# A written-out order for a fused attention and feed-forward kernel: both sketch loads first, and every engine's list rearranged

## The chip, the cores and the metric

The kernel runs on one core of one Trainium2 chip. The metric is the device time of one execution in microseconds (us). The engines are TensorE (PE), VectorE (DVE), ScalarE (ACT), GpSimd (POOL) and SyncE (SP), which only issues DMAs here; ACT issues a few as well.

## The reference

Polynomial-sketch attention, then a feed-forward block on its output. Batch 4, 4 heads, 1088 tokens, head size 32, sketch rank 8, model width 128, hidden width 512.

```python
def phi(x):                                  # sketch features, 8 x 8 = 64 for each token
    a = einsum('rd,bhsd->bhsr', S1, x)
    b = einsum('rd,bhsd->bhsr', S2, x)
    return einsum('bhsi,bhsj->bhsij', a, b).reshape(..., 64)
q_p, k_p = phi(q), phi(k)
kv  = einsum('bhsf,bhsd->bhfd', k_p, v)
z   = sum(k_p, axis=2)
num = einsum('bhsf,bhfd->bhsd', q_p, kv)
den = einsum('bhsf,bhf->bhs', q_p, z)[..., None] + 1e-06
x   = (num / den), heads side by side        # (4, 1088, 128)
xn  = (x - mean(x)) / sqrt(var(x) + 1e-06) * g_ln
out = x + maximum(xn @ w_ch1, 0) @ w_ch2
```

S1, S2, g_ln and the two weights reach the chip as 64-bit floats where numpy made them so, and are put together as 32-bit floats by integer and float steps on the engines (the `w_` steps).

## The kernel before

The kernel is a set of small steps (functions marked `@op`) and a text, `PROGRAM`, that lists 498 of them in order with their arguments. Nothing else schedules: each step issues its instructions to its engine's list when the text comes to it, so the text sets the order on every engine and in SP's DMA queue. An engine works through its list in order. A letter among the arguments names the engine (V for VectorE, A for ScalarE, G for GpSimd, S for SP); the last numbers of a step that uses TensorE are its banks of PSUM (0 to 7, in the tile `ALL`).

The four batches go through the same stages, and the text interleaves the stages of different batches.

- **Opening.** `ld_s` loads the two sketches into `s_raw` (8 rows), `ld_w` the weights, `ld_g` the norm's gain. `c_ones`, `c_small` (`one`, `m896`), `c_iota` (`row`, `head`), `c_masks` (six VectorE instructions that make `m32`, `m8` and `m2` from `row` and `head`), `c_ident`, `c_pads`, `c_vpad` and `c_rest` write constants. `fill n w z` is a matmul of ones with ones, w columns wide, whose result nobody reads.
- **Floats from 64 bits.** For sketch (0), first (1) and second weight (2): `w_ex`, `w_bits`, `w_e2`, `w_mant`, `w_low`, `w_e3`, `w_add` or `w_addlow`, and `w_mul`; for the sketch `s_heads` writes `s_f` at the end. `w_e2` and `w_mant` on ScalarE read `m896` and `one`. `sk` (L367, L369) turns the sketches on TensorE, `sk_8`, `sk_d`, `sk_2`, `sk_r`, `sk_q` copy them out. `fold` (L352) folds gain and mean into the first weight, `fold_cp` copies it.
- **Keys of a batch.** `ld S k b` loads, `turn_g` and `turn_r` (L419, L429) turn on VectorE, `k_feat` (L537) makes the features on TensorE, `k_tok` (L546) turns them back, `k_prod` (GpSimd) forms the 64 products in `kp`, `k_sum` (L561) and `k_zs` the sum z, `k_val` (L587) the product with v, and `k_vcp`, `k_spr` (L602), `k_rcp` bring it to `kvr`. `k_scr` (L456) and `k_sc` (L575) carry z into the sketches of q. `ld S k 2` reuses the buffer of batch 0, so it waits for `turn_r k 0`.
- **Queries of a batch.** Batch 0 goes through TensorE (`turn_p`, `turn_c`, `q_dir`, `q_cp`), the others through `turn_g`, `turn_r`, `q_feat` (L655) and `q_tok` (L664). `q_ac`, `q_den`, `q_rec`, `q_a2` and `q_prod` divide and form the products in `qp`; `q_turn0`, `q_turnr` and `q_turn` (L707, L712, L702) turn them to `qpT`.
- **Result of a batch.** `num` (L725) multiplies with `kvr`; `num_cp` and `num_r` copy its result to `xT` and `xTr`, `row_turn` (L787) turns it to rows, which go through DRAM (`row_wr`, `row_rd`) for the statistics (`st_bn`, `st_ag`, `st_pow`).
- **Feed-forward**, in pieces of 512 tokens (c = 0 to 7) and two of 128 (8, 9): `hid` (L834), `relu` (L842, L844), `sec` (L850), `fin`, or `fin_a` and `fin_g`, and `store`, `store_r`.

Of the kernel before, what the change touches and what calls it, by code (L numbers as in the profile page):

```python
# [25 lines left out]
def kernel(  # L26
# [880 lines left out]
    turn_p q 3 8 9; ld_h S q 0 8; k_feat 0 0 4; w_e3 V 1 0 512; fill 1 512 6; k_tok 0 0 4; c_cg G;
    k_sum 0 7; k_zs 0 7; c_ac 0; turn_p q 6 0 4; ld S k 1 0 34; ld S k 2 0 34; turn_r k 1; sk_r A 2;
    k_scr 7; w_mul G 1 0 512; ld_v S 0 2; turn_p q 1 4 8; sk_2 2; ld_vr S 0 0; turn_c A q 6 0 4;
    sk_dd G; turn_c A q 1 4 8; gram_d 7; q_dir 0 4 4; k_prod G 0 3 6; q_cp A 0 4 4 0 24; turn_g k 1  # L910
    0 4; sk_q 2; k_prod G 0 0 3; ld_v S 0 3; k_feat 1 0 1; turn_c V q 3 8 9; q_ac G 0 0 4; gram_r 7;
    q_dir 4 9 4; turn_g k 2 0 4; q_den 0 0 4; ld_v S 0 1; turn_r k 2; k_prod G 0 6 9; q_rec 0 0 4;
    k_tok 1 0 1; k_feat 2 2 3; q_a2 V 0 0 4; c_rest; q_cp A 4 9 4 0 24; q_ac V 0 4 9; k_sum 1 0;
    q_den 0 4 9; ld_vr S 0 1; k_tok 2 2 3; q_rec 0 4 9; ld_v S 0 0; k_val 0 0 9 5; q_prod G 0 0 2;
    ld S q 1 0 34; ld_v S 3 2; ld_vr S 1 0; ld_v S 1 2; fill 1 256 3; fold 1 0 256; q_prod V 0 2 4;
    k_zs 1 0; k_vcp A 0 5; k_spr 0 5; q_a2 G 0 4 9; fold 2 256 512; ld_w S 2 0 4; k_sc 1 3; k_rcp A
    0 5; q_turn0 0; num 0 0 4 6 7 4 5; fold_cp A 1 0 256; turn_r q 1; turn_g q 1 0 4; ld S k 3 0 34;
    k_sum 2 1; c_ac 1; num_cp A 0 0 0 4 6 7; k_sccp V 1 3; fill 1 256 3; c_vpad 1; num_cp V 0 1 0 4
    4 5; ld_v S 2 1; row_turn 0 1 4 5; q_prod G 0 6 9; hid 2 0 1 0 2; fold_cp A 2 256 512; hid 5 0 1
    2 4; relu A 5 0 1 2 4; row_turn 0 0 6 7; k_zs 2 1; q_turnr; relu A 2 0 1 0 2; q_prod G 0 4 6;  # L920
    q_turn0 1; ld_vr S 1 1; w_low A 2 0 512; q_feat 1 3 4 6 7; k_prod G 1 5 9; ld S q 2 0 34; k_sc 2
    1; ld_v S 1 0; q_tok 1 1 6 7; q_tok 1 0 3 4; row_wr S 0; turn_g k 3 0 4; hid 2 0 3 2 4; k_prod G
    1 0 5; hid 5 0 2 0 2; hid 0 0 0 0 2; relu A 2 0 3 2 4; relu A 5 0 2 0 2; hid 7 0 2 2 4; q_ac G 1
    0 4; num 0 4 9 2 3 5 6; ld_v S 1 1; relu A 7 0 2 2 4; relu V 0 0 0 0 2; num_cp A 0 1 4 8 5 6;
    num_cp V 0 0 4 8 2 3; hid 4 0 3 0 2; q_den 1 0 4; num_r V 0 2 3; w_bits V 2 0 512; w_ex V 2 0
    512; turn_r k 3; relu A 4 0 3 0 2; q_rec 1 0 4; q_ac G 1 4 9; w_mant A 2 0 512; hid 7 0 0 2 4;
    q_den 1 4 9; hid 0 1 1 0 4; ld_v S 1 3; w_e2 A 2 0 512; hid 4 1 2 0 4; w_add G 2 0 512; k_sccp V
    2 1; row_rd S 0; hid 1 1 0 0 4; ld_v S 2 0; sk_qq 2; relu A 7 0 0 2 4; row_turn 1 1 5 6; relu A
    4 1 2 0 4; relu A 0 1 1 0 4; row_turn 1 0 2 3; hid 3 1 3 0 4; k_feat 3 0 2; w_e3 V 2 0 512; relu
    A 3 1 3 0 4; q_a2 G 1 0 4; turn_r q 2; k_val 1 0 9 6; w_mul V 2 0 512; k_tok 3 0 2; k_sum 3 0;  # L930
    k_vcp A 1 6; q_prod G 1 0 4; q_rec 1 4 9; sec 5 0 2; k_zs 3 0; k_spr 1 2; st_bn 0; q_a2 G 1 4 9;
    k_sc 3 5; turn_g q 2 0 4; sec 6 0 1; q_turn 0 4; k_sccp V 3 5; relu A 1 1 0 0 4; ld S q 3 0 34;
    k_rcp A 1 2; st_ag 0; sec 7 1 0; ld_vr S 3 0; row_wr S 1; q_feat 2 2 3 1 4; sec 4 0 3; q_prod G
    1 4 9; sec 6 1 2; q_turn 4 9; q_tok 2 1 1 4; sec 7 1 1; st_pow 0; ld_v S 2 2; ld_vr S 2 1;
    row_rd S 1; fin_a 5 0 2; num 1 0 9 4 5 0 1; sec 7 1 3; k_prod G 2 5 9; q_tok 2 0 2 3; q_ac V 2 0
    4; q_den 2 0 4; num_cp A 1 0 4 8 4 5; row_turn 3 1 0 1; sk_qq 3; fin_a 4 0 3; ld_v S 3 0; num_cp
    V 1 1 4 8 0 1; row_turn 2 1 0 1; sec 2 0 0; row_turn 3 0 4 5; q_ac G 2 4 9; q_den 2 4 9; st_bn
    1; k_prod G 2 0 5; num_r A 1 0 1; fin_a 6 0 1; row_wr S 3; num_cp V 1 0 0 4 4 5; hid 3 3 1 0 4;
    num_cp A 1 1 0 4 0 1; row_pe 8 6; q_rec 2 0 4; q_a2 G 2 0 4; ld_vr S 2 0; hid 1 3 3 0 4; st_ag
    1; hid 0 3 2 0 4; fin_a 2 0 0; row_cp A 8 6; st_pow 1; fin_a 6 1 2; ld_v S 2 3; turn_r q 3;  # L940
    row_turn 2 0 4 5; relu A 3 3 1 0 4; fin_a 7 1 3; turn_g q 3 0 4; st_bn 8; hid 2 2 1 0 4; hid 5 2
# [6 lines left out]
    6 8 3 0 1; num 2 0 9 2 3 0 1; row_turn 4 1 0 1; sec 7 3 1; st_ag 8; relu A 6 8 3 0 1; row_turn 5
    1 0 1; row_turn 4 0 2 3; num_cp A 2 1 4 8 0 1; row_wr S 4; row_turn 5 0 2 3; sec 6 3 0; sec 7 3
    3; num_r A 2 2 3; st_pow 3; fin_a 6 3 0; st_ag 2; k_prod G 3 5 9; num_cp V 2 0 0 4 2 3; num_cp A  # L950
    2 1 0 4 0 1; num_cp A 2 0 4 8 2 3; k_val 3 0 9 5; fin_g G 1; q_feat 3 2 3 0 1; q_tok 3 1 0 1;
    st_pow 2; fin_a 5 2 2; q_tok 3 0 2 3; q_ac V 3 0 4; q_den 3 0 4; hid 4 4 3 0 4; k_vcp A 3 5;
# [57 lines left out]
```

## Time and profile before

| | |
|---|---|
| median of 3 runs | 103.19 us (102.77 to 103.45) |
| profiled execution | 103.05 us, of which the span from first to last instruction is 101.2 us |
| instructions | 3143 |
| TensorE matmul busy | 95.8 us, 95% of the span |
| VectorE, GpSimd, ScalarE busy | 73.2, 57.9, 38.8 us |
| DMA | 14.37 MB, mean 142 GB/s |
| granted TensorE clock | 1.00 throughout |

The profile comes from one execution. A row of the timeline gives start, duration, engine, line and operation, output and inputs, and in brackets the idle time of the engine before it with what ended that; rows of one line that follow one another are merged, with their count. A row of the chain gives start, duration and what ran. A row of the table by stretches gives the stretch, its length and then the busy time of each engine in it. "DMA to landing" is the time from a DMA's issue to its arrival.

### The profile page before, as it was taken

Reading aid. Unit: us, or ns where it says so; the run is one execution under the profiler, and the core shown is the slowest. Engines: PE = TensorE matmul, PEld = TensorE weight load, DVE = VectorE, ACT = ScalarE, POOL = GpSimd, SP = SyncE. Lnnn points to the kernel's source line nnn. Section 1 sums busy time; section 2 is a strip of 40 time slices with the busy share of each in tenths; the row PEclk is TensorE's granted clock in tenths of the full one; section 3 lists DMA queues with packets and bytes.
Section 4 is the critical chain, followed back from the end, with each engine's and each line's share of the span. In section 5 each row is a group of like instructions: output and inputs, shape, how many; then the busy total and the mean of one; then the engine's idle time right before and its main releaser. Section 6 shows DMA issues by size and latency. Waiting matters only on the chain.

```text
span 101.2 us, 3143 instructions
## 1 busy us (share of the span) xinstructions
PE 95.8 (95%) x1273; PEld 67.2 (66%) x1273; DVE 73.2 (72%) x213; ACT 38.8 (38%) x92; POOL 57.9 (57%) x80
## 2 busy tenths in 40 slices
...
GB/s 32 294 361 291 269 218 216 345 279 286 41 233 305 148 15 6 0 84 161 189 158 4 6 207 187 233 1 0 0 6 176 242 197 40 104 0 6 125 170 41
DMA packets 13119, 14.37 MB, mean 142 GB/s; under 512 B 2480, under 2 KB 10160, under 8 KB 13104
## 3 DMA queue, kind: packets, MB, share of 16 engines
...
q8 instruction: 10, 0.16, 0.7%
...
HBM read 9.84 MB, written 4.33 MB: 140 GB/s over the span
## 4 chain that ended last, share of the span: by engine, by line
PE 94%; DVE 1%; issue 1%; ACT 1%; ACTq 1%
PE ALL L850 31%; PE ALL L834 30%; PE ALL L257 8%; PE ALL L725 7%; PE ALL L587 4%; PE ALL L537 3%; PE ALL L621 2%; PE ALL L655 2%; PE ALL L438 1%; PE ALL L561 1%; PE ALL L602 1%; PE ALL L367 1%; ACTq L894 1%; DVE ones L196 0%; PE ALL L575 0%
## 5 line engine op out<-in xcount | busy, mean ns | idle before, releaser
L850 PEld LDWEIGHTS ALL<-w,hT 128*128 128x128 f32 x272 | 32.2, 192 | 4.8 <-issue 4.0
L850 PE MATMUL ALL<-w,hT 128*128 128x128 f32 x272 | 33.7, 277 | 0.0
L834 PE MATMUL ALL<-xT,w 128*128 128x512 f32 (+1 forms) x72 | 30.7, 552 | 0.0
L842 ACT ACTIVATE hT<-ALL 128x512 f32<-128x512 f32 (+2 forms) x34 | 15.8, 486 | 16.2 <-PE ALL L834 9.3
L834 PEld LDWEIGHTS ALL<-xT,w 128*128 128x128 f32 x72 | 12.3, 190 | 8.0 <-issue 5.0
L87 POOL TENSOR_TENSOR kp<-kf 128x768 f32<-128x768 f32 (+2 forms) x9 | 17.4, 1943 | 0.0
L87 POOL TENSOR_TENSOR qp<-a,fq 128x512 f32<-128x512 f32 (+3 forms) x7 | 13.8, 1979 | 3.2 <-DVE a L87 3.0
L818 POOL TENSOR_TENSOR va<-mv,eps 128x4 f32<-128x4 f32 (+1 forms) x10 | 2.0, 200 | 15.9 <-DVE mv L813 15.9
L868 ACT ACTIVATE ob<-ALL,rstd 128x128 f32<-128x128 f32 x20 | 6.9, 370 | 10.5 <-PE ALL L850 3.8
L257 PE MATMUL ALL<-ones 128*128 128x256 f32 (+1 forms) x18 | 9.3, 642 | 1.5 <-DVE ones L196 1.5
L820 POOL TENSOR_TENSOR rstd<-va,mhalf 128x4 f32<-128x4 f32 (+1 forms) x10 | 9.2, 923 | 2.3 <-DVE ob L863 1.6
L82 ACT COPY xT<-ALL 128x256 f32<-128x256 f32 x10 | 5.8, 648 | 10.2 <-PE ALL L725 8.0
L787 DVE STREAM_TRANSPOSE xh<-ALL 128x256 f32<-128x256 f32 x16 | 6.3, 421 | 4.4 <-issue 2.7
L844 DVE TENSOR_SCALAR hT<-ALL 128x512 f32<-128x512 f32 (+2 forms) x10 | 6.0, 604 | 3.9 <-PE ALL L834 3.9
L725 PE MATMUL ALL<-qpT,kvr 32*32 32x288 f32 (+2 forms) x320 | 7.8, 364 | 0.6 <-issue 0.4
L863 DVE SCALAR_TENSOR_TENSOR ob<-ALL,rstd,x 128x128 f32<-128x128 f32 x12 | 3.7, 343 | 6.1 <-PE ALL L850 5.4
L702 DVE STREAM_TRANSPOSE qpT<-qp 128x1024 f32<-128x1024 f32 (+1 forms) x6 | 8.0, 1348 | 0.0
L807 DVE BATCH_NORM_STATS2 st<-x 128x6 f32<-128x128 f32 x32 | 6.8, 273 | 0.0
L315 POOL TENSOR_TENSOR mant<-mant,low 128x512 f32<-128x512 f32 x2 | 2.5, 1271 | 7.2 <-ACT mant L298 7.2
L725 PEld LDWEIGHTS ALL<-qpT,kvr 32*32 32x32 f32 x320 | 4.1, 103 | 3.6 <-issue 1.0
L257 PEld LDWEIGHTS ALL<-ones 128*128 128x128 f32 x18 | 4.0, 250 | 3.7 <-DVE ones L196 1.5
L664 DVE STREAM_TRANSPOSE fq<-ALL 128x576 f32<-128x576 f32 x6 | 4.3, 763 | 2.6 <-PE ALL L655 2.4
...
## 6 DMA issues: line engine op xcount, KB each, us to landing
...
```

The lines of the kernel that those rows point to most:

```text
L87: by[eng].tensor_tensor(out=o, in0=a, in1=b, op=ALU.mult)
L257: pe.matmul(bank(z, 0, w), ones[:, 0:P], ones[:, 0:w], start=True, stop=True)
L702: dve.transpose(_ap(qpT, 0, P, 32 * u0, [[32, u1 - u0], [TW, 8], [1, 32]]), qp[:, H * F * u0 : H * F * u1])
L725: pe.matmul(bank(z[r], o, o + w)[D * h : D * h + D], kvr[b % 2][rows, DM * f + D * h : DM * f + D * h + D], qpT[rows, c : c + w], start=(f ...
L787: dve.transpose(_ap(xh[slot(c)], 0, P, 64 * n * i, [[32 * n, 2], [32, n], [1, 32]]), pair(z, P * (c % 2), [[32, n], [1, 32]]))
L807: dve.bn_stats(out=sts[slot(c)][:, 6 * t : 6 * t + 6], in_=row_ap(c, t))
L820: pool.tensor_tensor(out=rstds[slot(c)][:, 0:n], in0=vas[slot(c)][:, 0:n], in1=mhalf[:, 0:n], op=ALU.pow)
L834: pe.matmul(bank(z, 0, n), w1[:, P * j : P * (j + 1)], cols(c)[:, a : a + n], start=True, stop=True)
L842: act.activation(o, i, AF.Relu)
L844: by[eng].tensor_scalar(out=o, in0=i, scalar1=0.0, scalar2=None, op0=ALU.max)
L850: pe.matmul(bank(z, DM * t, DM * (t + 1)), h[:, 512 * j + P * t : 512 * j + P * (t + 1)], w2[:, DM * j : DM * (j + 1)], start=(j == 0), st ...
L868: act.activation(ob(c)[:, P * t : P * (t + 1)], bank(z, P * t, P * (t + 1)), AF.Copy, scale=rstds[slot(c)][:, t : t + 1])
```

## The change

Only the text `PROGRAM` changes. It lists the same 498 steps in a new order, with other banks. Some move to another engine: the load of the first sketch from ScalarE's queue to SP's, the product of the second weight from VectorE to GpSimd, a `q_a2` and a `q_prod` from VectorE to GpSimd, and a few copies and relus between ScalarE and VectorE. The head of the text before and now:

```diff
-    ld_s A 1; c_iota; c_small; ld_s A 0; c_ones; fill 1 512 7; fill 1 256 5; fill 1 256 4; c_vpad 0;
-    c_pads 0; c_masks; ld_w S 1 0 4; c_pads 1; w_ex V 1 0 512; w_low A 1 0 512; ld_g S; w_ex V 0 0
-    64; w_bits V 0 0 64; w_e2 A 0 0 64; fill 1 512 1; w_bits V 1 0 512; w_mant V 0 0 64; w_e3 V 0 0
...
+    c_pads 0; c_rest; c_vpad 0; c_vpad 2; c_ones; fill 1 512 2; c_ident; ld_s S 0; ld_s A 1; ld_w S
+    1 0 4; w_ex V 0 0 64; w_bits V 0 0 64; fill 1 512 4; c_iota; c_masks; fill 1 256 4; c_small;
+    w_mant V 0 0 64; c_ac 0; w_addlow V 0 0 64; ld S k 0 0 34; fill 1 256 6; ld_g S; w_low A 1 0
+    512; ld S k 1 0 34; w_bits V 1 0 512; w_e2 A 0 0 64; w_ex V 1 0 512; w_e3 V 0 0 64; w_mant A 1 0
```

**VectorE's list at the start.** `ex_108`, `bits_107` and `mant_110` belong to the sketch, `ex_113` and `bits_112` to the first weight; `bit` and `m` are the masks. Before:

```order
L200 MEMSET one 128x1
L201 MEMSET m_89 128x1
L196 MEMSET ones 128x512
L220 TENSOR_SCALAR bit_93<-row 128x4
L222 TENSOR_TENSOR m_86<-bit_93,head 128x4
L228 TENSOR_TENSOR m_85<-bit_95,head 128x2
L283 TENSOR_SCALAR ex_113<-w_raw 128x512
L283 TENSOR_SCALAR ex_108<-s_raw 8x64
L288 TENSOR_SCALAR bits_107<-s_raw 8x64
L288 TENSOR_SCALAR bits_112<-w_raw 128x512
L87 TENSOR_TENSOR s_f<-mant_110,ex_108 8x256
```

Now (three of the mask rows are left out in both):

```order
L196 MEMSET ones 128x512
L283 TENSOR_SCALAR ex_108<-s_raw 8x64
L288 TENSOR_SCALAR bits_107<-s_raw 8x64
L220 TENSOR_SCALAR bit_93<-row 128x4
L222 TENSOR_TENSOR m_86<-bit_93,head 128x4
L228 TENSOR_TENSOR m_85<-bit_95,head 128x2
L200 MEMSET one 128x1
L201 MEMSET m_89 128x1
L288 TENSOR_SCALAR bits_112<-w_raw 128x512
L283 TENSOR_SCALAR ex_113<-w_raw 128x512
L310 SCALAR_TENSOR_TENSOR ex_108<-s_raw,e_109 8x64
L87 TENSOR_TENSOR s_f<-mant_110,ex_108 8x256
```

The first two sketch instructions, which need the loaded `s_raw`, moved from behind the masks and the first weight's `w_ex` to the place behind the ones; masks and small memsets now stand behind them.

**VectorE's list between the turn of k's batch 2 and the first turn of the q products** (`qpT`). Before:

```order
L677 TENSOR_REDUCE den_143<-ac_100 128x16
L684 RECIPROCAL rden_145<-den_143 128x16
L546 STREAM_TRANSPOSE kf_134<-ALL 128x2x9x32
L87 TENSOR_TENSOR a_147<-fq,rden_145 128x128
L87 TENSOR_TENSOR ac_100<-fq 128x20x8
L546 STREAM_TRANSPOSE kf_133<-ALL 128x2x9x32
L87 TENSOR_TENSOR qp<-a_147,fq 128x512
L707 STREAM_TRANSPOSE qpT<-qp 128x4x4x2x32
```

Now, where `bits_117` and `ex_118` belong to the second weight:

```order
L546 STREAM_TRANSPOSE kf_134<-ALL 128x2x9x32
L87 TENSOR_TENSOR ac_100<-fq 128x16x8
L288 TENSOR_SCALAR bits_117<-w_raw 128x512
L677 TENSOR_REDUCE den_143<-ac_100 128x16
L283 TENSOR_SCALAR ex_118<-w_raw 128x512
L684 RECIPROCAL rden_145<-den_143 128x16
L87 TENSOR_TENSOR ac_100<-fq 128x20x8
L87 TENSOR_TENSOR a_147<-fq,rden_145 128x128
L87 TENSOR_TENSOR qp<-a_147,fq 128x512
L546 STREAM_TRANSPOSE kf_133<-ALL 128x2x9x32
L707 STREAM_TRANSPOSE qpT<-qp 128x4x4x2x32
```

Three instructions are new in this stretch: a `q_ac` of 16 columns (`ac_100`), which GpSimd had, and the second weight's `w_bits` and `w_ex`.

**TensorE's list around the first `num`** (L725). Before:

```order
L257 MATMUL ALL<-ones 128x256
L352 MATMUL ALL<-w1g,cg 128x256
L602 MATMUL ALL<-ident,kvc 128x128 x2
L352 MATMUL ALL<-w1g,cg 128x256
L575 MATMUL ALL<-zT,s2b 128x32
L725 MATMUL ALL<-qpT,kvr_138 32x128 x32
L561 MATMUL ALL<-kf_133 32x32 x9
L257 MATMUL ALL<-ones 128x256
L834 MATMUL ALL<-xT_149,w_123 128x256 x2
L655 MATMUL ALL<-qT_99,skq_103 32x288 x16
```

Now:

```order
L257 MATMUL ALL<-ones 128x256
L602 MATMUL ALL<-ident,kvc 128x128 x2
L575 MATMUL ALL<-zT,s2b 128x32
L561 MATMUL ALL<-kf_133 32x32 x9
L725 MATMUL ALL<-qpT,kvr_138 32x128 x32
L655 MATMUL ALL<-qT_99,skq_103 32x288 x16
L834 MATMUL ALL<-xT_149,w_123 128x256 x2
L575 MATMUL ALL<-zT,s2b 128x32
```

The two folds (L352) moved ahead of this piece, behind `q_dir`; the `k_sum` (L561) went from behind `num` to ahead of it, and one fill of 256 from behind it to a place between the first `k_feat` and `k_sum`; the `q_feat` (L655) now comes before the first `hid`.

On SP, the second weight's load moved from behind most of the v loads to the place behind `ld S k 2`, ahead of all v loads, and `ld S k 1` from behind the q loads to ahead of them.

More of the change, by code (lines that the diff above doesn't have):

```diff
@@ L907 @@
[L907 to L941, printed above, removed]
@@ L948 @@
[L948 to L952, printed above, removed]
@@ new lines @@
+    0 4; ld_vr S 0 1; q_cp A 4 9 5 0 24; fold 6 0 256; w_ex V 2 0 512; q_rec 0 0 4; k_sum 1 7; q_ac
+    V 0 4 9; q_a2 V 0 0 4; k_zs 1 7; k_prod G 0 3 6; k_feat 2 1 3; q_prod V 0 0 2; q_den 0 4 9; ld_v
+    S 0 0; fold_cp A 6 256 512; ld_vr S 0 0; ld S q 1 0 34; k_val 0 0 9 4; fill 1 256 5; k_tok 2 1
+    3; q_rec 0 4 9; k_vcp A 0 4; k_spr 0 4; k_rcp A 0 4; q_prod G 0 2 4; q_turn0 0; q_a2 G 0 4 9;
+    sk_qq 3; ld S k 3 0 34; k_sc 1 5; fold_cp A 6 0 256; k_sccp V 1 5; turn_r q 1; k_sum 2 7; num 0
@@ new lines @@
+    0 4 0 1 3 4; turn_g q 1 0 4; k_zs 2 7; ld_v S 1 3; q_feat 1 6 7 2 5; q_prod G 0 6 9; row_turn 0
+    0 0 1; num_cp V 0 0 0 4 0 1; num_cp A 0 1 0 4 3 4; q_prod G 0 4 6; w_e2 A 2 0 512; hid 1 0 2 0
+    2; ld S q 3 0 34; w_mant A 2 0 512; ld_v S 1 1; q_tok 1 1 2 5; q_turnr; c_ac 1; hid 0 0 1 0 2;
+    k_sc 2 2; ld_v S 1 0; relu A 1 0 2 0 2; q_turn0 1; k_prod G 1 5 9; q_tok 1 0 6 7; ld_vr S 1 1;
+    ld_v S 3 3; hid 5 0 3 0 2; relu A 0 0 1 0 2; hid 1 0 2 2 4; relu A 5 0 3 0 2; w_add G 2 0 512;
@@ new lines @@
+    0 0 0 2; row_wr S 0; hid 3 1 1 0 4; relu A 6 0 1 2 4; q_den 1 4 9; relu A 3 1 1 0 4; ld_vr S 2
+    0; q_rec 1 4 9; q_a2 G 1 4 9; q_rec 1 0 4; q_a2 G 1 0 4; q_prod G 1 4 9; ld_v S 2 2; sec 7 0 0;
+    hid 0 1 2 0 4; turn_g k 3 0 4; k_feat 3 3 6; ld_vr S 2 1; relu A 2 1 0 0 4; turn_r q 2; k_val 1
+    0 9 1; relu A 0 1 2 0 4; turn_g q 2 0 4; k_vcp A 1 1; k_tok 3 3 6; q_prod G 1 0 4; q_turn 4 9;
+    k_sum 3 0; q_feat 2 3 5 2 6; c_vpad 3; k_spr 1 1; sec 0 0 2; k_prod G 2 5 9; row_wr S 1; ld_v S
```

84 lines of the change are left out of this document (54 added, 30 removed).

## The prediction

> **What bounds the kernel now.** The page comes first: the engine shares and the chain that ended last.
>
> ```profile
> PE 95.8 (95%) x1273; PEld 67.2 (66%) x1273; DVE 73.2 (72%) x213; ACT 38.8 (38%) x92; POOL 57.9 (57%) x80
> PE 94%; DVE 1%; issue 1%; ACT 1%; ACTq 1%
> ```
>
> TensorE (PE) is busy for 95% of the span and makes up 94% of the chain. An order that keeps the same matmuls can therefore give or take only where PE idles. The table by stretches says where that is.
>
> ```profile
> 12.00:16.00 4.00, 3.92 (x73) 2.80 (x73) 4.00 (x10) 1.72 (x5) 3.80 (x11) 1.00 1.09 239
> 16.00:20.00 4.00, 3.72 (x123) 3.00 (x121) 3.96 (x9) 1.02 (x3) 3.56 (x6) 1.00 1.11 269
> 20.00:30.00 10.00, 9.63 (x196) 6.07 (x175) 8.66 (x23) 5.59 (x12) 6.50 (x6) 1.00 0.71 207
> 40.00:50.00 10.00, 10.00 (x173) 6.35 (x172) 8.90 (x27) 4.14 (x12) 5.88 (x8) 1.00 0.35 110
> ```
>
> After the stretch's length come PE's busy time, weight loads, VectorE (DVE), ScalarE (ACT) and GpSimd (POOL); the last column is the DMA traffic in GB/s. PE lacks 0.08 us in 12 to 16, 0.28 in 16 to 20 and 0.37 in 20 to 30, so 0.73 in all; from 30 us on it is full. VectorE is full as well from 12 to 20 us: there the two engines run neck and neck. What the new order loses before 30 us is thus not swallowed later, since no idle time follows that could take it up; and the most that it can win is 0.73 us plus something at either end.
>
> **The opening.** The timeline of the first 7 us, and the first row behind the fills in the chain:
>
> ```profile
> 0.73 0.93 ACTq L114 DMA_DIRECT2D s_raw<-in_S_dram  x2
> 0.80 0.06 DVE L200 MEMSET one<- 128x1 f32 x1 [0.80 <-PEq L994]
> 0.96 0.48 DVE L196 MEMSET ones<- 128x512 f32 x1
> 1.37 0.57 DVE L220 TENSOR_SCALAR bit<-row 128x4 int32<-128x4 int32 x1
> 1.50 5.49 PE L257 MATMUL ALL<-ones 128*128 128x512 f32 x8 [1.50 <-DVE ones L196]
> 2.83 0.16 DVE L228 TENSOR_TENSOR m<-bit,head 128x2 f32<-128x2 int32 x1
> 4.31 0.43 DVE L283 TENSOR_SCALAR ex<-w_raw 128x512 uint32<-128x512 uint32 x1 [1.33 <-DMA w_raw<-in_moe_w_ch_dram]
> 5.07 0.18 DVE L283 TENSOR_SCALAR ex<-s_raw 8x64 uint32<-8x64 uint32 x1 [0.32 <-DMA s_raw<-in_S_dram]
> 5.28 0.41 DVE L288 TENSOR_SCALAR bits<-w_raw 128x512 uint32<-128x512 uint32 x1
> 6.09 0.41 DVE L87 TENSOR_TENSOR s_f<-mant,ex 8x256 f32<-8x256 f32 x1
> 6.99 0.73 PE ALL L367 x4
> ```
>
> Four fills of ones occupy PE from 1.50 to 6.99, and only then come the sketch matmuls (L367). VectorE builds its masks from 1.37 to 2.99 while the first weight and the sketches are under way, and finishes the sketches at 6.09 + 0.41 = 6.50, half a microsecond before PE asks for them. An earlier sketch is worth nothing by itself: the fills end when they end.
>
> *First term.* In the new order the ones lead VectorE's queue. They start at 0.80, not 0.96, and so do the fills: **-0.16**, fills over at 6.83 (same widths in all).
>
> *Second term.* In the new order w_ex and w_bits of the sketches stand directly behind the ones, ahead of all masks, and the engine works in order: it now waits for both sketch loads with six mask instructions and two small memsets behind it, which the wait hid before. When do the loads land?
>
> ```profile
> g_raw<-in_moe_g_ln_dram SPq DMA_DIRECT2D x1, 0.5 KB, 3.6
> DMA to landing us min/median/max: 1.9/4.2/9.1
> DMA to landing us min/median/max: 5.0/5.9/9.0
> DMA to landing us min/median/max: 3.6/5.7/7.8
> ```
>
> The rows are those of g_raw and then, from the answers by tile, of the v loads, the k loads and the two weights. At the start of the run 0.5 KB took 3.6 us and the first weight (512 KB, the lowest of the last row) 3.6 as well. I take 3.6 for the sketches: 0.73 + 3.6 = 4.33. The bounds are 1.9, the quickest v load, and 5.07 - 0.73 = 4.34 for the second sketch load of before, which stood behind the first. From the first sketch instruction to the end of the last, before needed 6.50 - 5.07 = 1.43 us. To it come the masks: 1.94, the first one's end, to 2.99 is 1.05 for five of them, and 0.16 for the first, as the last one's row has it (its own row of 0.57 began under the memset of ones; if it is that long again, 0.4 more). Then the two memsets (0.09, from 0.80 to 0.89), and w_ex of the first weight, which used to run ahead and now runs in between: 0.43 less 0.08, since independent instructions here overlap by that much (1.44, the end of the ones, less 1.37). That is 3.08, and 4.33 + 3.08 = 7.41. With 0.1 to reach PE, the sketch matmuls start at 7.5: PE waits 7.5 - 6.83 = **+0.67**. The wait is nothing if the loads land before 3.65, that is within 2.9 us, and at the upper bound it is 1.4.
>
> The Trainium skill, "DMA: Bandwidth & Descriptors", section "Anatomy of one DMA — SWDGE (gpsimd) path", gives a fixed 2.0 us for a DMA and bytes at 436 GB/s on top, for the GpSimd path. If this held for these queues, the sketches would be there at some 2.7 us and the second term would be zero (the first rival); the row of g_raw, 3.6 us for 0.5 KB, speaks against it.
>
> **From the sketches to the first num.** The chain rows of PE, and VectorE's rows for k's head 2 up to the first turn of the q products (L707), which the first num (L725) waits for:
>
> ```profile
> 7.79 0.20 DVE L429 STREAM_TRANSPOSE kT<-kn 128x64 f32<-128x64 f32 x1
> 7.96 0.63 PE ALL L257 x2
> 10.50 0.31 PE ALL L561 x17
> 16.10 1.08 PE ALL L587 x72
> 17.92 0.43 PE ALL L352 x2
> 13.18 1.22 DVE L419 STREAM_TRANSPOSE kT<-kn 128x1024 f32<-128x1024 f32 x1
> L87 DVE TENSOR_TENSOR ac<-fq 128x128 f32<-128x128 f32 x2 | 0.7, 357 | 0.1
> 17.98 1.25 DVE L707 STREAM_TRANSPOSE qpT<-qp 128x1024 f32<-128x1024 f32 x1
> 19.37 0.41 PE ALL L725 x6
> ```
>
> *PE's side.* Before, 19.37 - 6.99 = 12.38 us lie between the two, 0.36 of them idle. The new order brings one more fill of 256 (0.63) and a third k_sum (0.31) ahead of num; they are taken from behind it. PE arrives at 7.5 + 12.38 - 0.36 + 0.94 = 20.46.
>
> *VectorE's side.* The load of k's batch 2 goes into the buffer of batch 0 and waits on SP for turn_r k 0. That ended 7.99 - 6.50 = 1.49 after the sketches; now 7.41 + 1.49 = 8.90. With the quickest k landing, 5.0 us (before it was issued at about 7.97 and used at 13.18 without a wait, so 5.2 at most), it is there at 13.95, and VectorE has only 0.3 us of small work more than it needs until then. On SP everything behind that load moves along, the second weight first and the seven v loads after it. k_val 0 (L587) needs those: it stood at 16.10 and comes 0.51 (first two terms), 0.63 (the fill) and 0.86 (two folds of 0.43, now ahead of it) later, at 18.1. The 1.6 MB up to them, from 8.95 on at the 239 GB/s of 12 to 16 us, are moved by 15.7, and by 17.6 with the quickest load's 1.9 on top: I cost them at nothing, with half a microsecond of cover. From this turn to the end of L707 before took 19.23 - 13.18 = 6.05 us. New in the stretch are q_ac of 128 columns (from GpSimd: 0.36) and w_bits and w_ex of the second weight (0.41 and 0.43), each less 0.08 of overlap: 0.96. So L707 ends at 13.95 + 6.05 + 0.96 = 20.96, and num starts 0.14 later, as before, at 21.1. PE waits 21.1 - 20.46 = **+0.64** here, in place of the **-0.36** of before.
>
> **Behind the first num.** PE's fill and k_sum used to stand between num and the first hid, and covered the copy of num's result; now only q_feat does.
>
> ```profile
> 20.95 0.62 DVE L84 COPY xT<-ALL 128x256 f32<-128x256 f32 x1 [0.39 <-PE ALL L725]
> 21.41 0.75 DVE L787 STREAM_TRANSPOSE xh<-ALL 128x256 f32<-128x256 f32 x2
> 21.75 1.07 PE ALL L834 x4
> 22.75 0.77 PE L655 MATMUL ALL<-qT,skq 32*32 32x288 f32 x32
> 26.06 0.37 issue
> ```
>
> num ended at 20.82; the copy began 0.13 later, took 0.62, and hid followed 0.18 after it: 0.93. The new order puts one row_turn (0.75 / 2) ahead of the copy, less 0.08: about 1.22, against 0.77 of q_feat. That is **+0.45**. The 0.37 at 26.06, where PE stood before the second num, goes: the two turns needed there come some 2.4 us behind the copy (q_tok, q_turnr, q_turn0), and PE has five hid and a k_sc, 2.6 us, to do: **-0.37**.
>
> **The rest.** From 30 us on I forecast no change. PE's list is the same work and ends with the same sec 7 9 0 and its fin:
>
> ```profile
> 97.67 0.36 DVE ob L863
> 98.04 0.55 SPq L894 DMA_DIRECT2D out_dram<-ob  x1
> ```
>
> Now fin 1 7 0 and a store of 128 KB stand between them. Both are ready when sec 7 9 0 ends, so SP has that store issued (0.4 to 0.5 us) about when the last fin is over, at 0.4: at most 0.1, costed at nothing. Several places there have under half a microsecond to spare by the same kind of count, so a loss of 0 to 0.5 belongs in the range. The second weight's product moves from VectorE to GpSimd, which is 57% busy and has the time.
>
> **The sum**, against the profiled execution's 103.05: -0.16 + 0.67 + 0.64 - 0.36 + 0.45 - 0.37 = +0.87, so **103.9 us**. That execution lies 0.14 under the median of the runs shown, 103.19; the forecast is 0.7% above that median. About 1% is what a measurement of this kernel can tell from no change.
>
> **The rivals.** (a) *The sketch loads land within 2.9 us*, alone at the head of their queues. Then PE starts them at 6.83. VectorE is held by k's first load, which landed at about 6.6 before and does so again, so the load of batch 2 keeps its 7.97 and lands at about 13.0; L707 ends at 20.0, num starts at 20.12, and PE, there at 19.79, waits 0.33 where it waited 0.36. -0.16 + 0.33 - 0.36 + 0.45 - 0.37 is 102.9, and with no wait for num's copy 102.5. For it: nothing stands ahead of either load. Against it: 3.6 us for 0.5 KB in the same first microseconds. Chance 0.24. To be faster by over 1%, below 102.16, takes all of the 0.73 and the 0.16, or fills at the start that take less than their 5.49: 0.09.
>
> (b) *The second weight stops VectorE.* Its load used to be issued at 13.79 and was needed at 28; now it follows the load of k's batch 2, at about 9.4, and w_bits stands on VectorE at about 13.95 + 1.15 + 0.15 + 0.65 + 0.3 = 16.2, with ACT's w_low ahead of the copy that q_ac needs. With the 7.8 us of before it lands at 17.2 and the whole stretch to num is 1.0 later: 104.9. It decides from a landing over 6.8 us. For it: the only row for this load. Against it: in that row several loads stood ahead of it, now one does. Chance 0.22.
>
> (c) *The place of the loads decides nothing*: the masks read what GpSimd's iota writes, and iota now follows pads, six tiny memsets and the identity.
>
> ```profile
> 2.34 0.28 POOL L215 COPY ident<-ident 8x128 f32<-8x128 f32 x1
> 15.73 0.21 POOL L252 MEMSET skq<- 128x8 f32 x4
> ```
>
> GpSimd had iota, pads and identity done at 2.62; four of the six memsets take 0.21. That makes some 3 us, 1.3 us before the landing that I take: the masks would start late through GpSimd only if the loads landed at under 2.3 us. No price, and no chance of its own.
>
> **How the numbers follow.** Forecast 103.9, own range 103.3 to 104.5, chance 0.48. Rival (a), 102.2 to 103.3, 0.24 with the 0.09 below that in it. Rival (b), 104.5 to 105.4, 0.22. Beyond that, losses after 30 us: 0.06. The range of 102.6 to 105.2 leaves out some 0.2: most of the 0.09, the last case, and a little of (b). Slower by over 1% is above 104.22: the top of the forecast's own range, 0.10, with (b) and the last case, 0.38. Faster by over 1% 0.09; within 1% 0.53.
>
> **What the changed profile would show.** The first fill at about 1.34; ex<-s_raw on VectorE with a long wait for the DMA, ending at about 4.3; s_f ending at about 7.4; L367 on PE at about 7.5 with PE idle ahead of it; num at about 21.1; a wait of 0.4 to 0.5 before the first hid. The forecast fails if ex<-s_raw starts before 3.6, if VectorE waits for w_raw at 16 us, or if PE idles after 30 us.

## The result: 1.0% faster, where 0.7% slower was forecast

| | before | after |
|---|---|---|
| median of the runs beside each other | 103.32 us (102.77 to 103.68) | 101.89 us (101.51 to 102.67) |
| ratio, 95% interval | | 0.990 (0.985 to 0.994) |
| profiled execution, span | 103.05, 101.2 | 101.51, 99.7 |

A second comparison of the same two kernels gave 0.986 (0.980 to 0.991). The forecast was 103.9 with a range of 102.6 to 105.2; the sign was wrong too. Medians in this document are over all executions of a kernel, while ratios and their intervals leave out those more than 1.5% above its fastest, most of which ran at a lower mean clock. The page and the table by stretches of the kernel after:

```profile
PE 94.6 (95%) x1273; PEld 67.2 (67%) x1273; DVE 72.2 (72%) x213; ACT 38.0 (38%) x89; POOL 59.9 (60%) x83
```
```profile
16.00:20.00 4.00, 3.99 (x148) 2.67 (x159) 3.95 (x13) 1.39 (x5) 2.85 (x4) 1.00 0.80 294
20.00:30.00 10.00, 9.53 (x185) 6.04 (x182) 9.00 (x22) 5.42 (x13) 9.94 (x10) 1.00 0.74 203
```

The span is 1.5 us shorter, but PE's visible idle time fell only from 0.73 us to 0.48 (none in 12 to 16 us, then 0.01 and 0.47 in the two rows). PE's *busy* time fell by 1.2 us, from 95.8 to 94.6, for the same 1,273 matmuls. So most of the gain lies inside what the page calls busy. The opening of the kernel after, from its timeline:

```profile
0.72 0.41 SPq L114 DMA_DIRECT2D s_raw<-in_S_dram  x1
1.43 5.49 PE L257 MATMUL ALL<-ones 128*128 128x512 f32 x8 [1.43 <-DVE ones L196]
2.29 0.70 DVE L283 TENSOR_SCALAR ex<-s_raw 8x64 uint32<-8x64 uint32 x1 [0.91 <-DMA s_raw<-in_S_dram]
6.07 0.41 DVE L87 TENSOR_TENSOR s_f<-mant,ex 8x256 f32<-8x256 f32 x1
6.85 0.38 PE L367 MATMUL ALL<-ident,s_f 8*128 8x8 f32 x1
```

The sketches are there at 2.29, 1.57 us after their issue. The sketches' floats are done at 6.48, and PE goes from its fills to the sketch matmuls without a wait. What holds the floats until then is the first weight: its `w_bits` stands on VectorE between the sketch instructions, and VectorE waited 0.65 us for that load, until 4.88. The first num and the first hid:

```profile
19.88 1.06 PE L725 MATMUL ALL<-qpT,kvr 32*32 32x128 f32 x64
21.23 0.78 PE L655 MATMUL ALL<-qT,skq 32*32 32x288 f32 x32 [0.29 <-DVE zT L569]
22.19 1.10 PE L834 MATMUL ALL<-xT,w 128*128 128x256 f32 x4 [0.18 <-ACT e L293]
```

PE reaches num at 19.88 and does not wait for the turn L707, which was done at 19.73. It then stands 0.29 and 0.18 us before q_feat and hid.

The same matmuls take longer before. These are the first num and the hid behind the second num in the kernel before, then the hid behind the second num after:

```profile
19.37 1.44 PE L725 MATMUL ALL<-qpT,kvr 32*32 32x128 f32 x64 [0.22 <-ACT w L82]
27.50 1.56 PE L834 MATMUL ALL<-xT,w 128*128 128x256 f32 x5
```
```profile
25.93 2.42 PE L834 MATMUL ALL<-xT,w 128*128 128x256 f32 x8
```

The first num counts as 1.44 us of busy time before and 1.06 after. Where the time went is seen in PE's weight loads. First before, from the first num to the second, then the second num after (start, busy time, line, shape, count, and in brackets the idle time of the loading side and what ended it):

```profile
19.34 0.17 PEld L725 LDWEIGHTS ALL<-qpT,kvr 32*32 32x32 f32 x7 [0.31 <-ACT w L82]
19.81 0.74 PEld L725 LDWEIGHTS ALL<-qpT,kvr 32*32 32x32 f32 x57 [0.29 <-issue]
20.74 0.27 PEld L561 LDWEIGHTS ALL<-kf 128*32 128x32 f32 x18 [0.20 <-issue]
21.05 0.30 PEld L257 LDWEIGHTS ALL<-ones 128*128 128x128 f32 x2
21.69 0.73 PEld L834 LDWEIGHTS ALL<-xT,w 128*128 128x128 f32 x4 [0.34 <-ACT xT L82]
22.75 0.23 PEld L655 LDWEIGHTS ALL<-qT,skq 32*32 32x32 f32 x32 [0.33 <-issue]
23.45 0.30 PEld L575 LDWEIGHTS ALL<-zT,s2b 128*128 128x128 f32 x2 [0.47 <-issue]
23.67 1.60 PEld L834 LDWEIGHTS ALL<-xT,w 128*128 128x128 f32 x8
25.60 0.14 PEld L725 LDWEIGHTS ALL<-qpT,kvr 32*32 32x32 f32 x4 [0.33 <-ACT hT L842]
26.42 0.67 PEld L725 LDWEIGHTS ALL<-qpT,kvr 32*32 32x32 f32 x44 [0.69 <-issue]
```
```profile
24.83 0.85 PEld L725 LDWEIGHTS ALL<-qpT,kvr 32*32 32x32 f32 x64 [0.33 <-DVE qpT L707]
```

The kernel before halts twice *inside* a num, behind its 7th weight load (0.29 us) and behind the 4th of the second num (0.69), and the profile shows nothing that it waits for ("issue"). The second num took 27.50 - 25.60 = 1.90 us from its start to the next hid; in the kernel after it took 25.93 - 24.83 = 1.10. Between the two halts lie 57 + 18 + 2 + 4 + 32 + 2 + 8 + 4 = 127 weight loads and as many matmuls: 254 instructions. The page counts ten packets on a queue of kind "instruction":

```profile
q8 instruction: 10, 0.16, 0.7%
```

That is 16 KB each. If these are TensorE's 2,546 loads and matmuls, there are some 255 to a packet. This gave **theory 1**: TensorE's instructions come in blocks over the same DMA engines as the data; while these are full, a block comes late, and PE halts at its border. **Theory 2**, the rival: the new order of the matmuls itself saves the time. **Theory 3**, for what is left: each change between matmuls of different tile shape (128\*128 of hid and sec, 128\*32 or 32\*32 of the groups between) costs PE time, and the new order has fewer.

### The profile page after: what moved, and what is told of

Read it like the earlier page. It is cut to its first block, busy times and chain, and to the rows that moved or that the text cites. A ratio compares the mean times of both kernels' runs of the same rounds, so it can differ in the third digit from the quotient of the medians.

```text
span 99.7 us, 3140 instructions
## 1 busy us (share of the span) xinstructions
PE 94.6 (95%) x1273; PEld 67.2 (67%) x1273; DVE 72.2 (72%) x213; ACT 38.0 (38%) x89; POOL 59.9 (60%) x83
## 4 chain that ended last, share of the span: by engine, by line
PE 94%; ACT 1%; DVE 1%; issue 0%; DVEq 0%
PE ALL L850 31%; PE ALL L834 30%; PE ALL L257 8%; PE ALL L725 7%; PE ALL L587 5%; PE ALL L537 3%; PE ALL L621 2%; PE ALL L655 1%; PE ALL L438 1%; PE ALL L561 1%; PE ALL L602 1%; PE ALL L352 1%; PE ALL L367 1%; ACT xT L82 1%; PE ALL L575 1%; DVE ones L196 0%
## 5 line engine op out<-in xcount | busy, mean ns | idle before, releaser
L850 PE MATMUL ALL<-w,hT 128*128 128x128 f32 x272 | 33.1, 276 | 0.0
L87 POOL TENSOR_TENSOR qp<-a,fq 128x1024 f32<-128x1024 f32 (+3 forms) x8 | 14.8, 1857 | 2.1 <-ACT w L82 1.8
L844 DVE TENSOR_SCALAR hT<-ALL 128x512 f32<-128x512 f32 (+1 forms) x11 | 6.1, 572 | 4.9 <-PE ALL L834 3.8
L702 DVE STREAM_TRANSPOSE qpT<-qp 128x1280 f32<-128x1280 f32 (+1 forms) x6 | 8.1, 1359 | 1.6 <-POOL qp L87 1.6
L725 PE MATMUL ALL<-qpT,kvr 32*32 32x288 f32 (+2 forms) x320 | 7.0, 364 | 0.0
L87 POOL TENSOR_TENSOR a<-fq,rden 128x160 f32<-128x160 f32 (+1 forms) x6 | 2.6, 435 | 5.0 <-DVE rden L684 4.5
L725 PEld LDWEIGHTS ALL<-qpT,kvr 32*32 32x32 f32 x320 | 3.9, 103 | 2.4 <-ACT hT L842 0.8
```

Of the source, the lines that this page charges most:

```text
L87: by[eng].tensor_tensor(out=o, in0=a, in1=b, op=ALU.mult)
L702: dve.transpose(_ap(qpT, 0, P, 32 * u0, [[32, u1 - u0], [TW, 8], [1, 32]]), qp[:, H * F * u0 : H * F * u1])
L725: pe.matmul(bank(z[r], o, o + w)[D * h : D * h + D], kvr[b % 2][rows, DM * f + D * h : DM * f + D * h + D], qpT[rows, c : c + w], start=(f ...
L850: pe.matmul(bank(z, DM * t, DM * (t + 1)), h[:, 512 * j + P * t : 512 * j + P * (t + 1)], w2[:, DM * j : DM * (j + 1)], start=(j == 0), st ...
```

## The experiments

### Fewer loads in flight, in the order of before

```diff
-    ld_v S 3 2; ld_vr S 1 0; ld_v S 1 2; ld_v S 2 1;
-    ld_vr S 1 1; ld S q 2 0 34; ld_v S 1 0;
...
     row_wr S 0;
+    ld_vr S 1 0; ld_v S 1 2; ld_vr S 1 1; ld_v S 1 0;
...
     ld_v S 1 3;
+    ld S q 2 0 34; ld_v S 2 1; ld_v S 3 2;
```

> Kernel before; only seven input loads of SyncE that nobody needs before 28 us are issued later (behind the first row write, at about 22 us), so that the DMA engines should be quiet from about 18 to 22 us. All other engines keep their order. Theory 1 (TensorE's own instruction blocks of 16 KB come late because data loads fill the DMA engines): the two halts inside num, 0.29 us at 19.5 and 0.66 us at 25.8, shrink to under 0.1 us each, and the time falls by 0.6 to 0.9 us, to a ratio of 0.991 to 0.994 against before. Theory 2 (the gain of the change comes from the new order of TensorE's operations alone): both halts stay, ratio 0.997 to 1.003.

Measured: 102.51 us, ratio **0.9925** (0.988 to 0.997). Weight loads of both nums, and the stretch in which the second block moved:

```profile
19.91 0.74 PEld L725 LDWEIGHTS ALL<-qpT,kvr 32*32 32x32 f32 x57 [0.16 <-issue]
25.70 0.85 PEld L725 LDWEIGHTS ALL<-qpT,kvr 32*32 32x32 f32 x64 [0.33 <-ACT hT L842]
```
```profile
20.00:22.00 2.00, 2.00 (x81) 1.38 (x79) 1.74 (x5) 0.64 (x1) 2.00 (x3) 1.00 0.06 21
```

The second halt is gone and the first about halved, to 0.16, where under 0.1 was expected of each; not one instruction of TensorE, VectorE, ScalarE or GpSimd was moved. The DMA engines were busy 6% of the time over 20 to 22 us (last column but one), where before had 114%. Theory 1 holds; theory 2 cannot explain this 0.8 us. The 0.16 that is left is not a late block: by the trace's packet records that block was there at 17.79, 2.1 us before PE went on. Its cause stays open.

### The same order, shifted along the instruction stream

```diff
-    fill 1 512 7;
+    fill 4 128 7;
```

> Kernel before; the first dummy matmul of 512 columns is cut into four of 128, which adds six instructions at the head of TensorE's stream and moves everything behind them by six places. Theory 1 (a halt lies at the border of an instruction block, 256 instructions apart): the two halts come six instructions, that is three weight loads, earlier in the same operations: the first stretch of num's weight loads, x7 before, becomes x4, and that of the second num, x4 before, becomes x1 or nothing. A rival by which the halt belongs to the operation or to its data keeps x7 and x4. The time stays within 0.4 us of before.

Measured: 103.59 us (one run), 0.5 over the 103.10 of before beside it, where at most 0.4 was expected. The weight loads of the first num, and of the hid ahead of the second, which then ran in one piece from 26.97:

```profile
19.15 0.10 PEld L725 LDWEIGHTS ALL<-qpT,kvr 32*32 32x32 f32 x1 [0.31 <-ACT w L82]
19.69 0.79 PEld L725 LDWEIGHTS ALL<-qpT,kvr 32*32 32x32 f32 x63 [0.44 <-issue]
23.59 1.17 PEld L834 LDWEIGHTS ALL<-xT,w 128*128 128x128 f32 x6
26.34 0.30 PEld L834 LDWEIGHTS ALL<-xT,w 128*128 128x128 f32 x2 [1.58 <-DVE kT L419]
```

x1 and "nothing", not x4 and x1: one fill is two loads and two matmuls, so the cut added 12 instructions, not 6. With that the halts lie just where they must: the first after 7 - 6 = 1 load of num, the second 4 - 6 = -2, two loads of hid before num begins. The halts belong to places in the instruction stream, not to num. The releaser named for the second (kT) is not its cause, since a hid reads xT and w only. And as the second border is now reached earlier while the block comes when it did (PE goes on at 26.34, before at 26.42), that halt is 1.58 us.

### More loads in flight, in the order of after

```diff
     ld_v S 1 3;
+    ld S q 2 0 34; ld_v S 1 1; ld_v S 1 0; ld_v S 3 3; ld_v S 1 2; ld_v S 2 2;
...
     ld S q 3 0 34;
-    ld_v S 1 1; ld_v S 1 0; ld_v S 3 3; ld_v S 1 2; ld S q 2 0 34; ld_v S 2 2;
```

> Kernel after; only six input loads of SyncE, which stood behind the load of q batch 3 and were issued from 21.5 us on, are issued ahead of it, at about 16 us, so that the DMA engines should stay full through 20 to 22 us, where they were at 6%. Theory 1 (late instruction blocks): an idle stretch of 0.3 to 0.9 us with no releaser comes back inside TensorE's narrow matmuls between 22 and 27 us, and the gain over before shrinks from 1.3 us to 0.3 to 0.9 us (ratio against before 0.992 to 0.997). Theory 2 (order of operations alone): no such stretch, ratio 0.987 to 0.992 as for after.

Measured: 102.97 us, ratio 0.995 (0.990 to 1.000). The time lies where theory 1 had put it, though the interval reaches to that of after. The weight loads of the second num and of the hid behind it:

```profile
24.95 1.03 PEld L725 LDWEIGHTS ALL<-qpT,kvr 32*32 32x32 f32 x64 [0.33 <-DVE qpT L707]
26.23 1.59 PEld L834 LDWEIGHTS ALL<-xT,w 128*128 128x128 f32 x8 [0.25 <-issue]
```

The num took 26.23 - 24.95 = 1.28 us, after 1.10. The 0.18 is a halt behind its 4th load, where before halts too, but it is less than the 0.3 that was expected at the least. The DMA queues show why, in the stretch of 20.0 to 21.2 us of after and then in 20.0 to 22.4 and 22.45 to 23.8 of this kernel:

```profile
q8 instruction: 1, 0.02, 5.5%
q1 hardware_dynamic: 11, 0.01, 3.2%
```
```profile
q1 hardware_dynamic: 292, 0.72, 100.5%
...
q8 instruction: 1, 0.02, 5.7%
```

The block that after fetched by 21.2 came by 23.8 with the data queue full, 2.6 us later. But its border lies in the second num, behind 24.95: almost in time. The traced execution took 101.83 us, no more than after, so where the others lose 1 us is not shown. The expectation thus failed on the size of the halt, and the next pair moves the border.

### Late block and early border together

```diff
-    fill 1 512 2;
+    fill 4 128 2;
...
-    fill 1 512 4;
+    fill 4 128 4;
...
-    fill 1 256 4;
+    fill 2 128 4;
...
-    fill 1 256 6;
+    fill 2 128 6;
```

Once alone on after (the control), once with the early loads of the experiment above.

> Kernel after; four dummy matmuls at the head are cut into twelve shorter ones of the same columns in all, which adds 32 instructions ahead of everything else on TensorE. It is the control for the next kernel. Theory 1 (instruction blocks): the border that lay inside the second num of batch 0 moves 32 instructions earlier, into the first hid at about 22.3 us; the block behind it has landed by 21.1 us, so the halt there is at most 0.3 us. Ratio against before 0.987 to 0.994. Theory 2 (order of operations alone): 0.987 to 0.992, no halt.

> Both at once: kernel after with six input loads issued ahead of the load of q batch 3, so that the DMA engines stay full over 20 to 24 us, and with 32 instructions more at the head, so that a block border falls into the first hid at about 22.3 us instead of the second num at 24.95. With the early loads alone the block landed at 23.7 us, in time for the border there. Theory 1 (a block comes late under data loads, TensorE stands when it reaches the border first): a halt of 1.5 to 2.7 us at the first hid, where 32 extra instructions alone give at most 0.3 us; the time is 1 to 2.5 us over that of after, ratio against before 1.000 to 1.015. Theory 2 (order of operations, or the data themselves): no halt over 0.3 us, ratio 0.990 to 0.997.

Measured: the control 101.80 us, ratio 0.9885 (0.981 to 0.996), no halt. Both together: **106.94 us** (four executions, 104.9 to 108.1). The weight loads of the first hid, and PE in one stretch (length, PE busy, granted clock, DMA share, GB/s), both of the kernel with both edits:

```profile
22.24 0.30 PEld L834 LDWEIGHTS ALL<-xT,w 128*128 128x128 f32 x2 [0.68 <-ACT e L293]
25.60 0.71 PEld L834 LDWEIGHTS ALL<-xT,w 128*128 128x128 f32 x2 [3.07 <-issue]
```
```profile
24.00:26.00 2.00, 0.40 (x2) 0.56 1.09 254
```

PE stands for 3.07 us between one hid and the next, released by nothing that the profile shows, and goes on at 25.60, 1.3 us after the stretch in which the block came (22.7 to 24.3, with the data queue at 109%). Either edit alone gives no such halt. Expected were 1.5 to 2.7 us; the halt was longer. The time rose by 5.1 us over the control, and even the quickest execution is 3.1 us over it, since the granted clock also fell to 0.50 from about 24 to 31 us; the halt had begun at the full clock. Theory 1 is shown from both sides.

The packet records of the traces say more. In the six longer halts (two each in before and in the shifted kernel, this one, and one in the kernel with late sketches below), PE goes on 1.2 to 1.5 us after the block's packet has ended. And a packet starts behind the border before its own: 0.4 us after that border in after, where the data queue was near empty (19.6, by the count of loads, to 20.0), and 4.2 us after it in before, with the queue full (19.8 to 24.0). So no more than one block is kept ahead here.

### The change's headline: the place of the sketch loads

Kernel before with the two loads of after, and kernel after with the loads of before:

```diff
-    ld_s A 1; c_iota; c_small; ld_s A 0;
+    ld_s S 0; ld_s A 1; c_iota; c_small;
```
```diff
-    ld_s S 0; ld_s A 1; ld_w S 1 0 4;
+    ld_s A 1; ld_s A 0; ld_w S 1 0 4;
```

> Kernel before; only the two sketch loads are placed as in after (one heads SyncE's queue, one ScalarE's). If the place of the sketch loads itself brings the gain, the ratio is 0.988 to 0.993. If, as the dummy matmuls up to 6.8 us hide the sketches on either placement, it brings nothing, the ratio is 0.997 to 1.003, the sketches land at about 2.3 us, and the first sketch matmul stays at 6.9 to 7.0 us.

> Kernel after; only the three first loads are placed as in before: the first weight heads SyncE's queue, both sketches go out on ScalarE's. If the place of the loads matters to the new order, whose VectorE reads a sketch first of all, the second sketch lands at about 5.1 us as in before and not by 2.3, the sketches' floats are ready at 8.2 to 8.6 us and not at 6.5, the first sketch matmul starts 1.3 to 1.7 us later, and the time rises by 0.5 to 1.5 us: ratio against before 0.994 to 1.004. If the place decides nothing: first sketch matmul at 6.7 to 6.9, ratio 0.986 to 0.992.

Measured: in before, 103.42 us, ratio 1.005 (1.001 to 1.009): no gain, rather a small loss, whose cause stays open. In its trace VectorE reads the sketches at 5.18 as ever, behind the first weight. In after, **104.77 us**, ratio 1.006 (1.000 to 1.0125): the whole gain lost, by the median some more. Rows of this second kernel, VectorE's first, then PE's, then PE's loads, and the granted clock over 11 to 12 us (last but two):

```profile
5.15 0.18 DVE L283 TENSOR_SCALAR ex<-s_raw 8x64 uint32<-8x64 uint32 x1 [3.77 <-DMA s_raw<-in_S_dram]
8.09 0.58 PE L367 MATMUL ALL<-ident,s_f 8*128 8x8 f32 x4 [1.36 <-DVE s_f L87]
23.12 0.21 PEld L561 LDWEIGHTS ALL<-kf 128*32 128x32 f32 x13 [1.05 <-issue]
```
```profile
11.00:12.00 1.00, 1.00 (x3) 0.50 0.96 373
```

The sketch lands at 5.15 again, and since this order has all masks behind it, PE stands 1.36 us, and its sketch matmuls come 1.24 us later than in after. Behind that come a half clock for some 3 us and a halt of 1.05 us at a block border. The DMA engines were idle during this halt (share 0.01 or less from 21 to 24 us); the packet, delayed by the data ahead, had ended at 21.85. The mean clock lay below 0.99 in 11 of the 12 executions of this kernel and in all four of the one with the 3 us halt. The twelfth kept its clock and took 102.75 us, still 1.0 over the 101.78 of after beside it. So the place of the loads is worth nothing to the old order, and the new order cannot do without it: the VectorE work behind the landing is real (5.15 to 7.94, so 2.79 us, where I had counted 3.08); only the landing was early.

### Changes of tile shape

On TensorE alone, sec groups are moved between narrow groups of the kernel after: two in the first kernel, five in the second.

```diff
     k_val 1 0 9 1;
...
+    sec 0 0 2;
     k_sum 3 0; q_feat 2 3 5 2 6;
...
+    sec 4 1 0;
     k_spr 1 1;
-    sec 0 0 2; sec 4 1 0;
```
```diff
-    sec 7 0 0;
...
     k_feat 3 3 6;
+    sec 7 0 0;
     k_val 1 0 9 1;
+    sec 0 0 2;
     k_sum 3 0;
+    sec 4 1 0;
     q_feat 2 3 5 2 6;
+    sec 7 1 1;
     k_spr 1 1;
-    sec 0 0 2; sec 4 1 0; sec 7 1 1;
...
     q_feat 3 1 5 3 6;
+    sec 2 2 1;
     k_val 3 0 9 0;
...
-    sec 2 2 1;
```

> Kernel after; on TensorE alone two of the sec groups that followed k_spr of batch 1 are moved between k_val and k_sum and between q_feat and k_spr, so that one run of narrow matmuls becomes three. Theory 3 (each change from wide matmuls to narrow ones and back costs TensorE about 0.1 us on either side, and after has five such places fewer than before, worth 0.5 us): two more places cost 0.35 to 0.45 us, ratio against before 0.993 to 0.996, in the trace 0.3 us or more on the sec and the narrow groups from 32 to 42 us. Rival: the changes cost nothing, and the place of the groups is free; ratio 0.987 to 0.991.

> Kernel after; on TensorE alone five sec groups are moved between narrow groups (k_feat, k_val, k_sum, q_feat and k_spr of batches 3, 1, 2 and 1, and q_feat and k_val of batch 3), so that there are five more changes from wide matmuls to narrow ones and back, as many as before has over after. The kernel with two more such places was 0.20 us longer in the trace from the start of k_val of batch 1 to that of num of batch 1 (8.12 us for 7.92), half of what was expected there. Theory 3 in that smaller form (0.1 us a place): five places cost 0.4 to 0.6 us, ratio against before 0.989 to 0.995, where after had 0.986 and 0.990. Rival: the changes cost nothing beyond the trace's rounding, 0.985 to 0.990, and the end of TensorE's work is within 0.2 us of that of after.

Measured: with two 101.73 us, ratio 0.987 (0.982 to 0.9915), not told apart from after and in the range expected if the changes cost nothing; with five 102.76 us, ratio 0.995 (0.992 to 0.998), where after had 0.990 (0.985 to 0.994) and 0.986 (0.980 to 0.991), with medians of 101.89 and 101.78. PE's timeline, of after, then of the kernel with two, then of that with five:

```profile
31.75 0.72 PE L537 MATMUL ALL<-kT,sk 64*32 64x288 f32 x16
34.87 5.52 PE L850 MATMUL ALL<-w,hT 128*128 128x128 f32 x48
40.32 1.60 PE L725 MATMUL ALL<-qpT,kvr 32*32 32x288 f32 x64
```
```profile
32.16 0.71 PE L537 MATMUL ALL<-kT,sk 64*32 64x288 f32 x16
33.95 1.16 PE L850 MATMUL ALL<-w,hT 128*128 128x128 f32 x8
35.04 0.38 PE L561 MATMUL ALL<-kf 128*32 128x32 f32 x18
...
36.05 1.16 PE L850 MATMUL ALL<-w,hT 128*128 128x128 f32 x8
37.04 0.38 PE L602 MATMUL ALL<-ident,kvc 128*128 128x128 f32 x2
...
40.93 1.60 PE L725 MATMUL ALL<-qpT,kvr 32*32 32x288 f32 x64
```
```profile
31.96 0.72 PE L537 MATMUL ALL<-kT,sk 64*32 64x288 f32 x16 [0.40 <-ACT hT L842]
42.01 1.60 PE L725 MATMUL ALL<-qpT,kvr 32*32 32x288 f32 x64
```

Six sec in a row take 40.32 - 34.87 = 5.45 us, 0.91 each. A sec with a narrow group on both sides takes 35.04 - 33.95 = 1.09. One between q_feat (32\*32) and k_spr, which is narrow too but of shape 128\*128, takes 37.04 - 36.05 = 0.99. So, as far as these rows tell, it is the change of shape that costs, about 0.1 us each time, not the narrow group. From k_feat to num the stretch took 8.57 us in after and 8.77 with two more changes: +0.20. With five it took 10.05, one sec (0.89) among it that stood ahead before: +0.59 for the four changes that lie there. That makes 0.10 to 0.15 a change. Theory 3 holds with half the price that I first wrote; the price comes from single traces. Not all that the five cost is of this kind: 0.40 is a wait for hT that this order added.

The Trainium skill, "TensorEngine Tiling (Array Packing)", section "Key Properties", says that changing the tiling mode drains TensorE. The rows agree in that each change costs time; they show the price, not the drain.

My count of "five fewer" was loose. By shapes in PE's timeline there are 16 changes from 28 us on before and 14 after (16 and 19 in these two kernels), and 19 ahead of 28 us in all four. Two changes are 0.2 to 0.3 us of the gain by this price.

### An attempt at a better version

In the first kernel VectorE issues the copy of num ahead of the row transpose; the second kernel also drops the last fill ahead of the sketches.

```diff
-    row_turn 0 0 0 1; num_cp V 0 0 0 4 0 1;
+    num_cp V 0 0 0 4 0 1; row_turn 0 0 0 1;
```
```diff
-    fill 1 256 6;
...
     sk 0;
```

> Kernel after; on VectorE the copy of num into xT is issued ahead of the row transpose of the same unit, so that the first hid should start at about 21.75 us and not at 22.19. If that wait of TensorE is a real loss, the time falls by 0.3 to 0.4 us, ratio against before 0.985 to 0.988. If the next wait (q_feat's features, the second num's qpT) takes its place, it stays at 0.988 to 0.991.

> Kernel after with the copy of num into xT ahead of the row transpose on VectorE (which alone gave 0.985), and without the last dummy matmul ahead of the first sketch matmul. The sketches' floats are ready at 6.48 us while the dummies end at 6.85, so the first sketch matmul should start at about 6.5 us. If that start is on the path, another 0.2 to 0.4 us goes: ratio against before 0.980 to 0.984. If TensorE then only waits longer for the turned keys and queries between 8 and 20 us, nothing more: 0.984 to 0.987.

Measured: 101.53 us, ratio **0.985** (0.980 to 0.990), and 101.52 us, ratio **0.980** (0.974 to 0.986). Rows of the first, then of the second kernel:

```profile
20.94 0.78 PE L655 MATMUL ALL<-qT,skq 32*32 32x288 f32 x32 [0.29 <-DVE zT L569]
21.81 1.10 PE L834 MATMUL ALL<-xT,w 128*128 128x256 f32 x4
```
```profile
6.39 0.58 PE L367 MATMUL ALL<-ident,s_f 8*128 8x8 f32 x4 [0.92 <-DVE s_f L87]
```

In the first, hid starts 0.38 us earlier than in after, as expected, but most of that is not the edit's. In this execution the four fills took 4.31 us for after's 5.49, the sketch matmuls started at 6.56 for 6.85, and PE came to q_feat at 20.94 for 21.23: 0.29 us were won ahead of num. From q_feat to hid it took 21.81 - 20.94 = 0.87, after 22.19 - 21.23 = 0.96. So the copy first wins 0.09 us: the 0.18 of wait goes, but hid still follows q_feat, which keeps its own 0.29 of wait. In the second kernel PE starts the sketches 0.46 earlier than after; there it waits 0.92 for s_f, and in the first, with the fill, it had waited 0.81, so the fill held up little in these two. A wait of 0.23 before num takes a part back. The intervals of both kernels overlap with those of after, so neither is told apart from it by its time.

## Why the prediction was wrong, point by point

**"The most that it can win is 0.73 us plus something at either end."** This step failed. It took "busy" for "at work". The halts inside num show in part as busy matmuls, and so do changes of shape; together they are some 1.0 us of the gain. What the profile had said is in the quoted 0.37 of "issue" at 26.06: a wait for nothing that the profile shows.

**The sign** failed by another step, the landing of the sketches: +0.67, and with it +0.64 at the first num, did not come. With the landing put right and all else as in the prediction, its own rival (a) comes to 102.9, slightly faster than before.

**The second num, -0.37.** The wait went, but not for the reason given. I read that "issue" as a wait for two turns, and argued that the turns would come in time. It was the tail of a halt that cost 1.90 - 1.10 = 0.80 us. With the 0.29 in the first num, some 0.7 us of halts lay hidden behind what I counted. The second went because SyncE in the new order stands at the load of q batch 3 until 21.1 us, so that hardly any data are under way when the block is fetched: an accident of the loads' order, which the prediction did not see coming. In the first num about half of the 0.29 was a late block; the 0.16 that stayed in the experiment is not.

**The sketches, +0.67.** The mechanism was right (masks behind the wait; 2.79 us of work in the kernel with late sketches, 3.08 counted); the landing was mis-sized: 3.6 us were taken from g_raw, 1.57 were measured. That is below my lower bound of 1.9. The 2.0 us by the Trainium skill, "DMA: Bandwidth & Descriptors", section "Anatomy of one DMA — SWDGE (gpsimd) path", would have been much nearer, though it is given for GpSimd's path. The load of g_raw was the second on SyncE's queue, behind the first weight's 512 KB; at the head of its queue a load of a few KB was quicker here. With it goes the wait: 0. That the floats then wait for the first weight (6.48, where a landing at 2.29 and 3.08 of work give 5.37) was in neither count.

**The first num, +0.64.** Failed in consequence. The load of k's batch 2 was issued at 7.79 and not at 8.95, L707 ended at 19.73 and not at 20.96. PE's own arrival, 20.46 less the 0.67, would be 19.79; 19.88 was measured. The -0.36 was right (0.01 of it stayed).

**The copy ahead of hid, +0.45.** hid came 22.19 - 20.94 = 1.25 us after num's end; 1.22 were forecast, and the mechanism was right. PE's idle time there was 0.47, of which 0.29 stood before q_feat, which I had taken as cover: it waited for zT. The experiment with the copy first won 0.09 back.

**The fills, -0.16.** Measured 0.07: the ones began at 0.89, not 0.80.

**Rivals.** The landing of (a) came true, its 102.9 did not: it had neither halts nor shapes, and its wait of 0.33 at num did not come. (b) did not decide. Its load was issued at 8.18 and had landed at 14.76, when ScalarE went on that had waited 0.68 us for it. That is 6.6 us, just under the 6.8 that I had named; VectorE did not wait.

**The sum as measured**, against 103.05: fills -0.07; idle time of PE from 12 to 30 us -0.25 (0.73 to 0.48); halts counted as busy, 0.29 and 0.80 less the idle 0.37, -0.72; two changes of shape, at the price above, -0.2 to -0.3. That is -1.24 to -1.34 of the -1.54. What the other 0.2 to 0.3 us are stays open.
